# Attention scores by 32 small matmuls instead of 8 padded ones, and a softmax that reads PSUM

## The chip, the cores and the metric

The kernel runs on one core of one Trainium2 chip. The metric is the device time of one execution in microseconds (us). Three executions were timed; times of two kernels that lie within 0.3% of each other (about 3.7 us here) can hardly be told apart.

## What is computed

Chunked attention with memory keys, then two gated feed-forward layers over the same 3072 tokens (4 sequences of 768, 8 heads of 64):

```python
for c in range(nc):                      # chunks of 32 queries
    l_start, r_end = max(0, c_start - 16), min(S, c_end + 8)
    k_full = concat(mem_k, k[l_start:r_end])     # 8 memory keys and up to 56
    scores = scale * q_c @ k_full.T
    a = exp(scores - max(scores)); a = a / (sum(a) + 1e-9)
    out[c] = a @ v_full
x = (sigmoid(x @ w_gate) * (x @ w_val)) @ w_out          # 512 -> 1536 -> 512
h = x @ w_in                                              # 512 -> 2048
g = (a0 + a1*h + a2*h*h + a3*h*h*h) / (1 + |b0|*|h| + |b1|*h*h + 1e-6)
y = g @ w_out2                                            # 2048 -> 512
```

A chunk of 32 queries sees at most 8 + 16 + 32 + 8 = 64 keys (KEYS). Two neighbouring chunks of one sequence share a window of 104 keys (WIN): memory, the context of both, memory again.

## The kernel before

**Tiling.** The tokens are handled in 24 tiles of 128 (index t). A tile has 8 heads and two groups g of 64 queries, each group two chunks. In the kernel before, one "set" is 128 query rows of the scores: for one pair of heads (r, 4 of them) and one g, two chunks c by two heads h by 32 queries. `attn_qk` makes a set with one matmul that contracts 128 rows, two heads of 64 features, over all 104 keys of the window; the host has laid out q so that each query column holds zeros in the other head's rows, so a tile's q is 512 KB. The 8 sets fill two PSUM tiles sp, four sets each. ScalarE then copies from each the 64 keys that belong to a chunk (lines 99 and 100, two copies of 64 rows by 4 x 64 for each PSUM tile) into the SBUF tile s. In the first and last tile of each sequence (every t with t % 6 equal to 0 or 5) GpSimd masks the keys that lie outside it.

**Softmax.** `attn_max` (VectorE: maximum over each 64 keys, then subtraction), `attn_exp` (ScalarE), `attn_sum` and `attn_mul` (VectorE, into a buffer with zeros outside the chunk's keys). `attn_t` transposes the 8 sets (tiles tp), `attn_pv` multiplies by the values in 16 matmuls with 64 weight columns, 64 moving columns and 104 rows (tile xp). All of these are plain float32, which the trace shows as two MATMUL records and two LDWEIGHTS records for each matmul of the source, except the transposes, which have one.

**Feed-forward layers.** They run on blocks of 512 tokens. Each large product is three float32r matmuls (hi by hi, hi by lo, lo by hi): `gate_val` (line 235, tile h), `out1` (line 267, tile acc), `h2` (line 316), `out2` (line 355). Weights arrive as raw 64-bit words, are converted by ScalarE and VectorE and split into hi and lo (`split_hi`, `split_lo`, line 222) during the first block, a step ahead of their use.

**Order.** Everything is written out by hand, and each engine works through its own queue in that order. First comes a prologue (lines 472 to 538): loads on the SyncE queue, attention of tiles 0 to 3, first weights. Then come 72 steps, one for each block j and inner tile f of the first layer: `gate_val` twice, `g_split`, then `attn_qk` and `attn_max` where the plan has them, then `out1` of the step before. Tiles 4 to 23 of attention are spread over these steps, two tiles at a time, and are all done after half of the run. PSUM has four rotating banks (pool ps) for h, sp, tp and xp, and four fixed ones for acc.

Of the kernel before, what the change touches and what calls it, by code (L numbers as in the profile page):

```python
# [39 lines left out]
def fused_kernel(ctx: ExitStack, tc: tile.TileContext, q, k, v, w1, w2, coef, x2d, w2d, out):  # L40
    """Chunked attention with memory keys, then two gated feed-forward layers.

    Float32 operands of the large products are split exactly into two float32r
    parts, hi + lo; each product is hi*hi + hi*lo + lo*hi, accumulated in float32.
    Activations stay transposed (features on partitions), so that each layer's
    result is the next one's moving operand.
    """
    nc = tc.nc
# [14 lines left out]

    # Attention weights between zeros: each chunk's keys within the window of two.
    a_buf = [const.tile([P, NSET, WIN], F32, name=f"a{i}") for i in range(2)]
# [7 lines left out]
    def ps(name):  # L73
        return psp.tile([P, 512], F32, tag="ps", name=name)

# [1 line left out]
    qs, ks, vs, s_sb, at_sb = {}, {}, {}, {}, {}  # L77

    def load_qk(t):
        u = qs[t] = wpool.tile([P, NSET, P], F32, tag="w", name=f"q{t}")  # L80
        nc.sync.dma_start(out=u, in_=q[t])
        u = ks[t] = wpool.tile([P, KW], F32, tag="w", name=f"k{t}")
        nc.sync.dma_start(out=u, in_=k[t])

    def load_v(t):
        u = vs[t] = wpool.tile([P, VW], F32, tag="w", name=f"v{t}")
        nc.sync.dma_start(out=u[0:WIN], in_=v[t])

    def attn_qk(t):
        qt = qs.pop(t)  # L90
        kt = ks.pop(t).rearrange("p (s w) -> p s w", s=NSET)
        s = tpool.tile([P, NSET, KEYS], F32, tag="t", name=f"s{t}")
        for half in range(2):
            sp = ps(f"sp{t}_{half}")[:, 0 : 4 * WIN].rearrange("p (s w) -> p s w", s=4)
            for i in range(4):
                j = 4 * half + i
                nc.tensor.matmul(sp[:, i], lhsT=qt[:, j], rhs=kt[:, j], start=True, stop=True)  # L97
            j = slice(4 * half, 4 * half + 4)
            nc.scalar.activation(out=s[0:64, j], in_=sp[0:64, :, 0:KEYS], func=ACTF.Copy)
            nc.scalar.activation(out=s[64:128, j], in_=sp[64:128, :, OFF1:WIN], func=ACTF.Copy)  # L100
        sv = s.rearrange("p (r g) w -> p r g w", g=2)
        if t % SB == 0:
            nc.gpsimd.memset(sv[0:64, :, 0, NMEM : NMEM + LEFT], MASKED)
        if t % SB == SB - 1:
            e = CTX - RIGHT + NMEM - OFF1
            nc.gpsimd.memset(sv[64:128, :, 1, e : e + RIGHT], MASKED)
        s_sb[t] = s

    def attn_max(t):
        s = s_sb[t]  # L110
        m = spool.tile([P, NSET, 1], F32, tag="m", name=f"m{t}")
        nc.vector.tensor_reduce(out=m[:, :, 0], in_=s, axis=AX.X, op=ALU.max)
        nc.vector.tensor_tensor(out=s, in0=s, in1=m.to_broadcast([P, NSET, KEYS]), op=ALU.subtract)

# [34 lines left out]
    def attn_pv(t, x, n0):  # L149
        vt = vs.pop(t)[0:WIN].rearrange("p (g e) -> p g e", g=2)  # L150
        ats = at_sb.pop(t)
        xp = ps(f"xp{t}").rearrange("p (r n) -> p r n", r=4)
        for j in range(NSET):
            r, g = divmod(j, 2)
            at = ats[j // 4][0:WIN].rearrange("p (s c h q) -> p s h c q", s=4, c=2, h=2)
            for h in range(2):
                e = (2 * r + h) * D
                nc.tensor.matmul(  # L158
                    xp[64 * h : 64 * h + 64, r, 64 * g : 64 * g + 64],
                    lhsT=vt[:, g, e : e + D],  # L160
                    rhs=at[:, j % 4, h],
                    start=True,
                    stop=True,
                )
        hi, lo = x[:, :, 0, n0 : n0 + P], x[:, :, 1, n0 : n0 + P]
        nc.scalar.activation(out=hi, in_=xp, func=ACTF.Copy)  # L166
        nc.vector.tensor_tensor(out=lo, in0=xp, in1=hi.bitcast(F32), op=ALU.subtract)  # L167

# [1 line left out]
    # Float64 arrives as raw 8-byte words and is rounded to float32 here. The high  # L170
    # word, scaled as a float32, has its exponent rebased and in place after a shift
    # by 3; the 3 bits that this frees take the low word, rounded without a carry:
    # within one unit of float32, exact for float32 values, and even on average.
    stage = {}
# [48 lines left out]

    # hi*hi, hi*lo, lo*hi
    TERMS = ((0, 0), (0, 1), (1, 0))

# [1 line left out]
    xt, gp, sgs = {}, {}, {}  # L228
# [57 lines left out]

# [1 line left out]
    x2f, x2, w2f, rat = {}, {}, {}, {}  # L288
# [21 lines left out]
    def h2(j, f):  # L310
        """The rational function's negative, split; the sign goes out with the result."""
        x, w = x2[j], wp[2, 2 * f]
        hp = ps(f"h2_{j}_{f}")
        for kt in range(KT):
            for i, (a, b) in enumerate(TERMS):
                nc.tensor.matmul(  # L316
                    hp,
                    lhsT=w[:, a, kt * P : (kt + 1) * P],
                    rhs=x[:, kt, b],
                    start=(kt == 0 and i == 0),  # L320
                    stop=(kt == KT - 1 and i == 2),
                )
        t, qq, hh = t2(f"t{j}_{f}"), t2(f"qq{j}_{f}"), t2("hh")
        nc.scalar.activation(out=t, in_=hp, func=ACTF.Identity, scale=cf[:, 3:4], bias=cf[:, 2:3])  # L324
        nc.scalar.activation(out=qq, in_=hp, func=ACTF.Abs, scale=cab[:, 0:1])
        nc.scalar.activation(out=hh, in_=hp, func=ACTF.Square)  # L326
        nc.vector.tensor_tensor(out=t, in0=t, in1=hp, op=ALU.mult)  # L327
        nc.vector.scalar_tensor_tensor(out=t, in0=t, scalar=cf[:, 1:2], in1=hp, op0=ALU.add, op1=ALU.mult)  # L328
        nc.vector.scalar_tensor_tensor(out=qq, in0=hh, scalar=cab[:, 1:2], in1=qq, op0=ALU.mult, op1=ALU.add)  # L329
        rat[j, f] = t, qq  # L330

    def recip2(j, f):
        # 1 / Q: the square of 1 / sqrt(Q) from the table, and one Newton step.
        t, qq = rat[j, f]
        y = t2("y")
        nc.scalar.activation(out=y, in_=qq, func=ACTF.Abs_reciprocal_sqrt, bias=qc[:, 0:1])  # L336
        nc.scalar.activation(out=y, in_=y, func=ACTF.Square)  # L337
        rat[j, f] = t, qq, y
# [31 lines left out]

# [1 line left out]
    NB1 = len(BLOCKS1)  # L372
# [45 lines left out]
    def at(si, *call):  # L418
        plan.setdefault(si, []).append(call)

    # Weights of the first layer: scaled three steps ahead, converted two, split one.
    for si, (j, f, c0, n) in enumerate(steps):
# [4 lines left out]
        if j == 0:  # L427
            at(si - 2, bits1, f)
            at(si - 3, scale1, f)
            if f > 2:  # L430
                at(max(si - 3, 0), load_w1, f)
    # Attention of later blocks, two tiles of 128 tokens at a time.
    for t in range(4, NBLK, 2):
        j, i = divmod(t, 4)
        s0 = (j - 1) * NF1 + (5 if i else 0)
        if j == 1:
            s0 = 5 if i else 2
        for o, u in ((0, t), (1, t + 1)):
            at(s0 + o - 2, load_qk, u)
            at(s0 + o, attn_qk, u)  # L440
            at(s0 + o + 1, attn_max, u)
            at(s0 + 3, attn_exp, u)
            at(s0 + o + 3, load_v, u)
            at(s0 + o + 3, attn_sum, u)
            at(s0 + o + 3, attn_mul, u)
            at(s0 + o + 4, attn_t, u)
            at(s0 + o + 5, pv, u)
    # Conversion of the second layer's weights.
    for i in range(2 * NF2):
# [6 lines left out]
    def weights2(k, n):  # L456
        """The next n units are loaded and the ones before split."""
        for i in range(k, k + n):
# [6 lines left out]
    W2_AHEAD = 2  # L465
    # The second layer's first PRE inner tiles come within the first layer's last
    # steps; its second product is LAG2 steps behind its first.
    PRE, LAG2 = 3, 5
    with tc.manual_schedule():
        # The first block's attention and first weights, ordered so that no engine's  # L470
        # queue waits long for another's.
        load_qk(0)
# [122 lines left out]
def _windows(k, mem):  # L595
    """[B, H, S // 64, WIN, D]: memory, the context of two chunks, memory."""
    import numpy as np
# [62 lines left out]
```

## Time and profile before

| | |
|---|---|
| three timed runs, us | 1234.36, 1236.14, 1237.49 (median 1236.14) |
| span of the profiled execution, us | 1234.2 |
| TensorE matmul busy | 1213.6 us (98%) |
| TensorE weight loads busy | 1010.7 us (82%) |
| VectorE busy | 905.8 us (73%) |
| ScalarE busy | 792.8 us (64%) |
| mean granted TensorE clock | 0.995 |

The span runs from the first to the last instruction of the one execution that was profiled, so nothing of its own lies around it but what the timed runs add: the median is 1.9 us above the span. A matmul's record includes its way through a pipeline, so that records overlap; what a matmul costs is read from start to start.

### The profile page before, as it was taken

Reading aid. Unit: us, or ns where it says so; the run is one execution under the profiler, and the core shown is the slowest. Engines: PE = TensorE matmul, PEld = TensorE weight load, DVE = VectorE, ACT = ScalarE, POOL = GpSimd, SP = SyncE. Lnnn points to the kernel's source line nnn. Section 1 sums busy time; section 2 is a strip of 40 time slices with the busy share of each in tenths; the row PEclk is TensorE's granted clock in tenths of the full one; section 3 lists DMA queues with packets and bytes.
Section 4 is the critical chain, followed back from the end, with each engine's and each line's share of the span. In section 5 each row is a group of like instructions: output and inputs, shape, how many; then the busy total and the mean of one; then the engine's idle time right before and its main releaser. Section 6 shows DMA issues by size and latency. Waiting matters only on the chain.

```text
span 1234.2 us, 16440 instructions
## 1 busy us (share of the span) xinstructions
PE 1213.6 (98%) x6240; PEld 1010.7 (82%) x6240; DVE 905.8 (73%) x1426; ACT 792.8 (64%) x1382; POOL 3.3 (0%) x19
## 2 busy tenths in 40 slices
PE   5899999999999999999999999999999999999998
PEld 5788888888888888888888888888888888888887
DVE  5889655747465656556566579998888898898885
ACT  5988455655565555555555588777677677767765
POOL 0000000000000000000000000000000000000000
PEclk8999999999999999999999999999999999999999
DMA  9864151325242514422163120010010100100000
GB/s 320 312 210 148 46 158 52 110 91 175 65 128 86 183 53 141 137 90 79 54 203 94 43 69 18 9 52 9 10 52 9 44 18 9 52 18 1 35 1 35
DMA packets 39319, 105.40 MB, mean 85 GB/s; under 512 B 4488, under 2 KB 4488, under 8 KB 39240
## 3 DMA queue, kind: packets, MB, share of 16 engines
q1 hardware_dynamic: 39240, 104.35, 26.3%
q8 instruction: 49, 0.80, 0.3%
q14 instruction: 30, 0.25, 0.1%
HBM read 83.36 MB, written 20.97 MB: 85 GB/s over the span
## 4 chain that ended last, share of the span: by engine, by line
PE 97%; DMA 1%; ACT 1%; DVE 0%; issue 0%; SPq 0%
PE h L235 32%; PE acc L355 21%; PE h L316 21%; PE acc L267 16%; PE sp L97 3%; PE tp L144 2%; PE xp L158 2%; DMA k<-k_in 1%; DVE x L167 0%; ACT at L146 0%; ACT st L187 0%; ACT st L188 0%; ACT s L117 0%; DVE a L131 0%; DVE r L124 0%
## 5 line engine op out<-in xcount | busy, mean ns | idle before, releaser
L235 PE MATMUL h<-x,wp 128*128 128x512 f32 x1728 | 414.3, 393 | 3.7 <-ACT x L166 3.0
L235 PEld LDWEIGHTS h<-x,wp 128*128 128x128 f32 x1728 | 322.9, 188 | 72.0 <-ACT x L166 3.2
L316 PE MATMUL h<-x,wp 128*128 128x512 f32 x1152 | 276.5, 389 | 0.0
L355 PE MATMUL acc<-wp,g 128*128 128x512 f32 x1152 | 275.9, 389 | 0.0
L355 PEld LDWEIGHTS acc<-wp,g 128*128 128x128 f32 x1152 | 216.3, 188 | 44.8
L316 PEld LDWEIGHTS h<-x,wp 128*128 128x128 f32 x1152 | 216.2, 188 | 44.8
L267 PE MATMUL acc<-g,wp 128*128 128x512 f32 x864 | 210.1, 392 | 0.0
L267 PEld LDWEIGHTS acc<-g,wp 128*128 128x128 f32 x864 | 160.8, 188 | 33.0
L253 ACT ACTIVATE g<-sg 128x512 fp32r<-128x512 f32 x72 | 45.5, 632 | 179.9 <-DVE sg L247 179.9
L324 ACT ACTIVATE t<-h,cf 128x512 f32<-128x512 f32 x96 | 74.7, 778 | 127.9 <-PE h L316 127.0
L222 DVE TENSOR_TENSOR wp<-wf,wp 128x512 fp32r<-128x512 f32 x216 | 136.2, 684 | 5.9 <-ACT wp L218 5.7
L247 DVE TENSOR_TENSOR sg<-sg,h 128x512 f32<-128x512 f32 x72 | 49.5, 687 | 123.8 <-PE h L235 103.6
L218 ACT ACTIVATE wp<-wf 128x512 fp32r<-128x512 f32 x216 | 121.1, 622 | 6.2 <-DVE c L199 4.0
L327 DVE TENSOR_TENSOR t<-t,h 128x512 f32<-128x512 f32 x96 | 65.8, 686 | 45.3 <-ACT hh L326 43.6
L244 ACT ACTIVATE sg<-h 128x512 f32<-128x512 f32 x72 | 43.0, 598 | 75.9 <-PE h L235 75.7
L254 DVE TENSOR_TENSOR g<-sg,g 128x512 fp32r<-128x512 f32 x72 | 49.9, 692 | 52.1 <-ACT g L253 52.1
L328 DVE SCALAR_TENSOR_TENSOR t<-t,cf,h 128x512 f32<-128x512 f32 x96 | 71.8, 748 | 3.4
L342 DVE SCALAR_TENSOR_TENSOR qq<-qq,y 128x512 f32<-128x512 f32 x96 | 65.8, 685 | 11.0 <-ACT y L337 11.0
L336 ACT ACTIVATE y<-qq,qc 128x512 f32<-128x512 f32 x96 | 69.9, 728 | 5.0 <-DVE qq L329 4.7
L329 DVE SCALAR_TENSOR_TENSOR qq<-hh,cab,qq 128x512 f32<-128x512 f32 x96 | 71.7, 746 | 0.0
L343 DVE SCALAR_TENSOR_TENSOR t<-t,cf,y 128x512 f32<-128x512 f32 x96 | 71.5, 745 | 0.0
L344 DVE SCALAR_TENSOR_TENSOR t<-qq,t 128x512 f32<-128x512 f32 x96 | 66.5, 692 | 3.3
(52 smaller groups left out, 1018.0 us busy)
## 6 DMA issues: line engine op xcount, KB each, us to landing
st<-w_in SPq DMA_DIRECT2D x68, 512.0 KB, 8.0
q<-q_in SPq DMA_DIRECT2D x24, 512.0 KB, 12.0
k<-k_in SPq DMA_DIRECT2D x24, 416.0 KB, 7.9
v<-v_in SPq DMA_DIRECT2D x24, 416.0 KB
w2d<-c SPq DMA_DIRECT2D x32, 256.0 KB, 2.1
w2f<-w2d SPq DMA_DIRECT2D x32, 256.0 KB, 3.2
x2d<-x2s SPq DMA_DIRECT2D x24, 256.0 KB, 2.8
x2f<-x2d SPq DMA_DIRECT2D x24, 256.0 KB
```

The source lines that it names most:

```text
L218: nc.scalar.activation(out=wp[key][:, 0], in_=src, func=ACTF.Copy)
L222: nc.vector.tensor_tensor(out=t[:, 1], in0=src, in1=t[:, 0].bitcast(F32), op=ALU.subtract)
L235: nc.tensor.matmul(pt, lhsT=w[:, a, kt * P : (kt + 1) * P], rhs=x[:, kt, b, c0 : c0 + n], start=(kt == 0 and i == 0), stop=(kt == KT - 1 a ...
L267: nc.tensor.matmul(acc[j][d][:, c0 : c0 + n], lhsT=w[:, a, d * P : (d + 1) * P], rhs=g[:, b, 0:n], start=(f == 0 and c0 == 0 and i == 0), ...
L316: nc.tensor.matmul(hp, lhsT=w[:, a, kt * P : (kt + 1) * P], rhs=x[:, kt, b], start=(kt == 0 and i == 0), stop=(kt == KT - 1 and i == 2),)
L324: nc.scalar.activation(out=t, in_=hp, func=ACTF.Identity, scale=cf[:, 3:4], bias=cf[:, 2:3])
L328: nc.vector.scalar_tensor_tensor(out=t, in0=t, scalar=cf[:, 1:2], in1=hp, op0=ALU.add, op1=ALU.mult)
L329: nc.vector.scalar_tensor_tensor(out=qq, in0=hh, scalar=cab[:, 1:2], in1=qq, op0=ALU.mult, op1=ALU.add)
L336: nc.scalar.activation(out=y, in_=qq, func=ACTF.Abs_reciprocal_sqrt, bias=qc[:, 0:1])
L343: nc.vector.scalar_tensor_tensor(out=t, in0=t, scalar=cf[:, 0:1], in1=y, op0=ALU.add, op1=ALU.mult)
L344: nc.vector.scalar_tensor_tensor(out=t, in0=qq, scalar=2.0, in1=t, op0=ALU.subtract, op1=ALU.mult)
L355: nc.tensor.matmul(acc[j][m], lhsT=g[:, a, m * P : (m + 1) * P], rhs=w[:, b], start=(f == 0 and i == 0), stop=(f == NF2 - 1 and i == 2),)
```

## The change

A set is now one chunk index of the tile by one head: 128 rows are (c, g, 32 queries), four strips of 32. `attn_qk` issues, for each head pair r, chunk strip i and head h, one matmul that contracts only the 64 rows of that head (rows 64h on), has 32 weight columns (the chunk's queries) and 64 moving columns (the chunk's own keys), and writes 32 partitions of the PSUM tile of that h. That is 32 matmuls for a tile in place of 8. The layout of q needs no zeros and halves to 256 KB for a tile.

In the 16 tiles that need no mask, `attn_max` reads both PSUM tiles directly: two maxima and two subtractions of 128 x 256 in place of one of each of 128 x 512, and the four ScalarE copies are gone. In the 8 tiles with a mask, two copies of 128 x 256 remain. `attn_max` of the later tiles stands in the step of their `attn_qk`, one step earlier than before. `attn_pv` issues the same 16 matmuls, in an order of loops that follows the new sets. Comments were dropped.

```diff
-        for half in range(2):
-            sp = ps(f"sp{t}_{half}")[:, 0 : 4 * WIN].rearrange("p (s w) -> p s w", s=4)
-            for i in range(4):
-                j = 4 * half + i
-                nc.tensor.matmul(sp[:, i], lhsT=qt[:, j], rhs=kt[:, j], start=True, stop=True)
-            j = slice(4 * half, 4 * half + 4)
-            nc.scalar.activation(out=s[0:64, j], in_=sp[0:64, :, 0:KEYS], func=ACTF.Copy)
-            nc.scalar.activation(out=s[64:128, j], in_=sp[64:128, :, OFF1:WIN], func=ACTF.Copy)
+        sps = [ps(f"sp{t}_{h}")[:, 0 : 4 * KEYS].rearrange("p (r w) -> p r w", r=4) for h in range(2)]
+        for r in range(4):
+            for i in range(4):
                 c, g = divmod(i, 2)
+                for h in range(2):
+                    d = slice(64 * h, 64 * h + 64)
+                    o = slice(32 * i, 32 * i + 32)
+                    nc.tensor.matmul(
+                        sps[h][o, r],
+                        lhsT=qt[d, r, o],
+                        rhs=kt[d, r, g, c * OFF1 : c * OFF1 + KEYS],
+                        start=True,
+                        stop=True,
+                    )
...
+        if edge(t):
+            for h in range(2):
+                nc.scalar.activation(out=sv[:, :, h], in_=sps[h], func=ACTF.Copy)
...
+        else:
+            sc_ps[t] = sps
...
+        for h in range(2):
+            nc.vector.tensor_reduce(out=mv[:, :, h, 0], in_=sps[h], axis=AX.X, op=ALU.max)
+        for h in range(2):
+            nc.vector.tensor_tensor(
+                out=sv[:, :, h], in0=sps[h], in1=mv[:, :, h].to_broadcast([P, 4, KEYS]), op=ALU.subtract
+            )
...
-            at(s0 + o + 1, attn_max, u)
+            at(s0 + o, attn_max, u)
```

On TensorE, around tile 4 (names: h_2 is `gate_val` of inner tile f = 2, acc is `out1` of the step before), this stood before:

```order
L235 MATMUL h_2_0_0_584<-x_280,wp_0_2_0_494 128x512 x12
L235 MATMUL h_2_1_0_602<-x_280,wp_0_2_1_496 128x512 x12
L97 MATMUL sp_0_626<-k_427,q_425 128x104 x4
L97 MATMUL sp_1_633<-k_427,q_425 128x104 x4
L267 MATMUL acc_0_548<-g_0_1_0_545,wp_0_1_2_433 128x512 x3
```

and this stands there now, with sp_0 and sp_1 taking turns 32 times where the dots are:

```order
L261 MATMUL h_2_0_0_672<-x_368,wp_0_2_0_582 128x512 x12
L261 MATMUL h_2_1_0_690<-x_368,wp_0_2_1_584 128x512 x12
L104 MATMUL sp_0_713<-k_515,q_513 32x64
L104 MATMUL sp_1_714<-k_515,q_513 32x64
...
L293 MATMUL acc_0_636<-g_0_1_0_633,wp_0_1_2_521 128x512 x3
```

The block stands at the same place; only its form is another.

On VectorE, in the prologue (tiles 1 and 2; m is the maximum, r the reciprocal sum, s the scores), this stood before:

```order
L112 TENSOR_REDUCE m_197<-s_163 128x8
L113 TENSOR_TENSOR s_163<-s_163,m_197 128x512
L112 TENSOR_REDUCE m_201<-s_178 128x8
L113 TENSOR_TENSOR s_178<-s_178,m_201 128x512
L124 TENSOR_REDUCE r_204<-s_163 128x8
```

and this stands there now:

```order
L135 TENSOR_REDUCE m_259<-sp_0_185 128x4
L135 TENSOR_REDUCE m_259<-sp_1_186 128x4
L137 TENSOR_TENSOR s_219<-sp_0_185,m_259 128x4x64
L137 TENSOR_TENSOR s_219<-sp_1_186,m_259 128x4x64
L135 TENSOR_REDUCE m_265<-sp_0_220 128x4
L135 TENSOR_REDUCE m_265<-sp_1_221 128x4
L137 TENSOR_TENSOR s_254<-sp_0_220,m_265 128x4x64
L137 TENSOR_TENSOR s_254<-sp_1_221,m_265 128x4x64
L150 TENSOR_REDUCE r_270<-s_219 128x8
```

VectorE now waits for TensorE itself there, in place of ScalarE's copies, and has four instructions for two.

## Rows read from the trace of the kernel before

**Rows 1.** The page: engines, and shares of the chain that ended last.
```profile
PE 1213.6 (98%) x6240; PEld 1010.7 (82%) x6240; DVE 905.8 (73%) x1426; ACT 792.8 (64%) x1382; POOL 3.3 (0%) x19
PE 97%; DMA 1%; ACT 1%; DVE 0%; issue 0%; SPq 0%
```

**Rows 2.** Busy time by stretch: start:end and length, each engine, PEclk, DMA share, GB/s.
```profile
0.00:20.00 20.00, 10.71 (x62) 10.60 (x62) 8.08 (x15) 7.84 (x17) 2.33 (x12) 0.93 0.91 319
40.00:100.00 60.00, 60.00 (x297) 50.23 (x297) 53.56 (x91) 53.69 (x98) 0.27 (x2) 0.99 0.69 234
140.00:600.00 460.00, 460.00 (x2643) 384.23 (x2642) 269.98 (x439) 254.84 (x456) 0.66 (x5) 1.00 0.33 104
```

**Rows 3.** Timeline of TensorE, 141 to 172 us: start, length, instructions merged.
```profile
141.83 2.88 PE L235 MATMUL h<-x,wp 128*128 128x512 f32 x12
144.64 1.15 PE L158 MATMUL xp<-at,v 104*64 104x64 f32 x32
145.72 3.02 PE L235 MATMUL h<-x,wp 128*128 128x512 f32 x12
148.57 2.88 PE L267 MATMUL acc<-g,wp 128*128 128x512 f32 x12
151.29 5.60 PE L235 MATMUL h<-x,wp 128*128 128x512 f32 x24
156.74 1.93 PE L97 MATMUL sp<-k,q 128*128 128x104 f32 x16
158.44 3.01 PE L267 MATMUL acc<-g,wp 128*128 128x512 f32 x12
161.29 5.60 PE L235 MATMUL h<-x,wp 128*128 128x512 f32 x24
```

**Rows 4.** The same timeline from 135 us, eight transposes and what follows them.
```profile
135.42 1.08 PE L144 MATMUL tp<-ident,a 128*104 128x128 f32 x8
136.26 3.01 PE L235 MATMUL h<-x,wp 128*128 128x512 f32 x12
```

**Rows 5.** TensorE's busy time and granted clock (PEclk, third) in three early stretches.
```profile
24.08:25.25 1.17, 1.17 (x32) 1.00 1.03 406
31.08:34.10 3.02, 3.02 (x97) 1.00 1.03 409
17.20:20.83 3.63, 3.63 (x18) 0.53 1.07 397
```

**Rows 6.** Timeline of TensorE in the first 60 us.
```profile
17.20 3.63 PE L97 MATMUL sp<-k,q 128*128 128x104 f32 x16 [3.72 <-DMA k<-k_in]
38.34 12.52 PE L235 MATMUL h<-x,wp 128*128 128x512 f32 x47 [0.73 <-DVE x L167]
```

**Rows 7.** Timeline of VectorE, 10 to 30 us; in brackets the idle time before.
```profile
10.21 0.69 DVE L112 TENSOR_REDUCE m<-s 128x8 f32<-128x512 f32 x1 [10.21 <-ACT s L100]
13.12 0.17 DVE L125 TENSOR_SCALAR r<-r 128x8 f32<-128x8 f32 x1
13.99 0.69 DVE L112 TENSOR_REDUCE m<-s 128x8 f32<-128x512 f32 x1 [0.46 <-ACT s L100]
15.58 0.69 DVE L112 TENSOR_REDUCE m<-s 128x8 f32<-128x512 f32 x1 [0.17 <-ACT s L100]
21.67 0.69 DVE L112 TENSOR_REDUCE m<-s 128x8 f32<-128x512 f32 x1 [0.97 <-ACT s L100]
23.44 0.69 DVE L124 TENSOR_REDUCE r<-s 128x8 f32<-128x512 f32 x1 [0.36 <-ACT s L117]
25.07 0.69 DVE L124 TENSOR_REDUCE r<-s 128x8 f32<-128x512 f32 x1 [0.50 <-ACT s L117]
26.12 2.75 DVE L131 TENSOR_TENSOR a<-s,r 64x512 f32<-64x512 f32 x4
```

**Rows 8.** The chain that ended last, its longest transfer; then ScalarE's copies by line.
```profile
5.45 11.62 DMA k<-k_in
...
L100 ACT ACTIVATE s<-sp 64x256 f32<-64x256 f32 x48 | 18.2, 380 | 0.6
```

More of the change, by code (lines that the diff above doesn't have):

```diff
@@ L74, in ps @@
         return psp.tile([P, 512], F32, tag="ps", name=name)
-    qs, ks, vs, s_sb, at_sb = {}, {}, {}, {}, {}
+    qs, ks, vs, s_sb, sc_ps, at_sb = {}, {}, {}, {}, {}, {}
     def load_qk(t):
-        u = qs[t] = wpool.tile([P, NSET, P], F32, tag="w", name=f"q{t}")
+        u = qs[t] = wpool.tile([P, 4, P], F32, tag="w", name=f"q{t}")
         nc.sync.dma_start(out=u, in_=q[t])
@@ L87, in load_v, with edge @@
         nc.sync.dma_start(out=u[0:WIN], in_=v[t])
+    def edge(t):
+        return t % SB in (0, SB - 1)
     def attn_qk(t):
         qt = qs.pop(t)
-        kt = ks.pop(t).rearrange("p (s w) -> p s w", s=NSET)
-        s = tpool.tile([P, NSET, KEYS], F32, tag="t", name=f"s{t}")
-        for half in range(2):
-            sp = ps(f"sp{t}_{half}")[:, 0 : 4 * WIN].rearrange("p (s w) -> p s w", s=4)
+        kt = ks.pop(t).rearrange("p (r g w) -> p r g w", r=4, g=2)
+        sps = [ps(f"sp{t}_{h}")[:, 0 : 4 * KEYS].rearrange("p (r w) -> p r w", r=4) for h in range(2)]
+        for r in range(4):
             for i in range(4):
-                j = 4 * half + i
-                nc.tensor.matmul(sp[:, i], lhsT=qt[:, j], rhs=kt[:, j], start=True, stop=True)
-            j = slice(4 * half, 4 * half + 4)
-            nc.scalar.activation(out=s[0:64, j], in_=sp[0:64, :, 0:KEYS], func=ACTF.Copy)
-            nc.scalar.activation(out=s[64:128, j], in_=sp[64:128, :, OFF1:WIN], func=ACTF.Copy)
[L101 to L107, printed above, removed]
+                c, g = divmod(i, 2)
+                for h in range(2):
[8 more added lines that the diff above has]
+                    )
+        s = s_sb[t] = tpool.tile([P, NSET, KEYS], F32, tag="t", name=f"s{t}")
+        sv = s.rearrange("p (r h) w -> p r h w", h=2)
+        if edge(t):
+            for h in range(2):
+                nc.scalar.activation(out=sv[:, :, h], in_=sps[h], func=ACTF.Copy)
+            if t % SB == 0:
+                nc.gpsimd.memset(s[0:32, :, NMEM : NMEM + LEFT], MASKED)
+            else:
+                e = CTX - RIGHT + NMEM - OFF1
+                nc.gpsimd.memset(s[96:128, :, e : e + RIGHT], MASKED)
+        else:
+            sc_ps[t] = sps
     def attn_max(t):
@@ L111, in attn_max @@
         m = spool.tile([P, NSET, 1], F32, tag="m", name=f"m{t}")
-        nc.vector.tensor_reduce(out=m[:, :, 0], in_=s, axis=AX.X, op=ALU.max)
-        nc.vector.tensor_tensor(out=s, in0=s, in1=m.to_broadcast([P, NSET, KEYS]), op=ALU.subtract)
+        if edge(t):
+            nc.vector.tensor_reduce(out=m[:, :, 0], in_=s, axis=AX.X, op=ALU.max)
+            nc.vector.tensor_tensor(out=s, in0=s, in1=m.to_broadcast([P, NSET, KEYS]), op=ALU.subtract)
+            return
+        sv = s.rearrange("p (r h) w -> p r h w", h=2)
+        mv = m.rearrange("p (r h) w -> p r h w", h=2)
+        sps = sc_ps.pop(t)
+        for h in range(2):
[4 more added lines that the diff above has]
+            )
     def attn_exp(t):
@@ L152, in attn_pv @@
         xp = ps(f"xp{t}").rearrange("p (r n) -> p r n", r=4)
[L153 to L164, printed above, removed]
+        for r in range(4):
+            at = ats[r // 2][0:WIN].rearrange("p (s c g q) -> p s g c q", s=4, c=2, g=2)
+            for g in range(2):
+                for h in range(2):
+                    e = (2 * r + h) * D
+                    nc.tensor.matmul(
+                        xp[64 * h : 64 * h + 64, r, 64 * g : 64 * g + 64],
+                        lhsT=vt[:, g, e : e + D],
+                        rhs=at[:, 2 * (r % 2) + h, g],
+                        start=True,
+                        stop=True,
+                    )
         hi, lo = x[:, :, 0, n0 : n0 + P], x[:, :, 1, n0 : n0 + P]
@@ L613 @@
     a = {n: np.asarray(x) for n, x in inputs.items()}
-    q = a["q"].reshape(B, 4, 2, SB, 2, 2, CH, D).transpose(0, 3, 2, 7, 1, 4, 5, 6)
-    qd = np.zeros((B, SB, 2, D, 4, 2, 2, 2, CH), q.dtype)
-    for h in range(2):
-        qd[:, :, h, :, :, :, :, h] = q[:, :, h]
+    qd = a["q"].reshape(B, 4, 2, SB, 2, 2, CH, D).transpose(0, 3, 2, 7, 1, 5, 4, 6)
     kd = _windows(a["k"], a["mem_k"]).reshape(B, 4, 2, SB, 2, WIN, D)
@@ L635 @@
     arrays = {
-        "q_in": qd.reshape(NBLK, P, NSET, P),
+        "q_in": qd.reshape(NBLK, P, 4, P),
         "k_in": kd.reshape(NBLK, P, KW),
```

## The prediction

> **What bounds the kernel now.** I read the page's engine lines and the chain that ended last first: TensorE is busy for 98% of the span and has 97% of that chain [rows 1]. Then the busy time by stretch: from 40 us on TensorE has no gap (60.00 of 60.00, 460.00 of 460.00), while VectorE and ScalarE are busy for 53.6 and 53.7 of 60 us up to 100 us, and for little over half of the time after it [rows 2]. So two stages have different rules. In the prologue, up to 38.34 us, where the dense matmuls start [rows 6], transfers and then VectorE and ScalarE set the pace. After it, what TensorE spends per attention tile is added to the time, and what the other engines save is worth nothing. Twenty of the 24 tiles have their scores in that second stage, so the price of a score block on TensorE, start to start, is the first thing to work out.
>
> **The price of a score block before.** Dense work alone: 24 h matmuls start at 151.29 and the sp block at 156.74, so 5.45 us for 24, or 0.227 us each [rows 3]. From 151.29 to 161.29 there are 24 h, one sp block and 12 acc: 10.00 - 36 x 0.227 = 1.83 us for one sp block with its changes of form. Inside it 16 records take 156.74 to 158.44, 0.106 us each. A record has 128 weight columns and 104 moving ones. A transpose has 104 weight columns and 128 moving ones and costs (136.26 - 135.42) / 8 = 0.105 us [rows 4]. So a column costs about 0.83 ns in float32 on either side, loading and streaming overlap, and the larger of the two sets the pace.
>
> **The price after.** No row has a matmul of 64 rows and 32 columns. The nearest is xp: 64 weight columns and 64 moving ones, into alternating halves of the output partitions, two records for each matmul, as the new one. Three blocks in a row, 96 records, cost 3.02 us and one block of 32 costs 1.17, both at the full clock (granted 1.00, the 2.4 GHz level) [rows 5]; the 97th record counted there is the end of the one before: (3.02 - 1.17) / 64 = 28.9 ns a record, 57.8 ns a matmul. By 0.83 ns a column one record streams for 53 ns, two 107 ns; a matmul that adds only 58 therefore overlaps half of itself with its neighbour. I read this as: the second record of a matmul must wait until the first has streamed its 64 columns through the same part of the array (53 ns), the next matmul, in another part, starts a few ns after the second, and starts keep their order. The whole xp block, from 141.83 to 148.57 with 24 h around it, costs 6.74 - 5.45 = 1.29 us [rows 3], so 1.29 - 16 x 0.0578 = 0.37 us go into entering and leaving the small form.
>
> The new block has the same 64 moving columns and the same pair of records on the same part of the array; only its neighbours are spread over eight parts and not two, and its load is 32 columns, which was not the slower side. If starts keep their order the eight parts help no more than two do. I take 57.8 ns: 32 x 0.0578 + 0.37 = 2.22 us in place of 1.83, +0.39 us a tile, **+7.8 us** for 20 tiles. The matmul count grows fourfold, and the work per matmul falls by less.
>
> Bounds for that price. From below, full independence of the eight parts: each has 4 matmuls of two records, 8 x 53 ns = 0.43 us, and 0.79 us with the 0.37, -1.04 a tile. From above, each load and stream one after the other, 27 + 53 ns a record: 64 x 0.080 + 0.37 = 5.5 us, +3.7 a tile; the xp rows, which would then cost 107 ns a record, speak plainly against that. For entering and leaving, sp itself shows that it can be less (1.83 - 16 x 0.106 = 0.13 us for the 128-column form) and nothing shows that it can be more; that gives +0.15 to +0.39 a tile at the same rate.
>
> **The prologue.** There the change helps. The chain before runs through the arrival of tile 3's k at 17.07 (5.45 + 11.62) [rows 8]. Four q of 512 KB lie ahead of it in the queue, and now four of 256 KB: 1.05 MB less, at 319 GB/s (mean of 0 to 20 us [rows 2]) to 406 GB/s [rows 5] 2.6 to 3.3 us earlier. Whether VectorE can use it: before its last multiplications for tiles 2 and 3 (26.12) it idled, after its first maximum at 10.21, for 0.46, 0.17, 0.97, 0.36 and 0.50 us behind ScalarE's copies or the exponentials that were queued behind them [rows 7], 2.46 us together; the first k comes 0.6 us earlier too (256 KB at 406 GB/s). For tiles 1 to 3 the copies go (four of 0.38 us each tile [rows 8]) and with them those waits. Against that stand four VectorE instructions for two in three tiles. A 128 x 512 reduction takes 0.69, an instruction on 128 x 8 0.17 [rows 7], so half the size is about 0.43: 4 x 0.43 - 2 x 0.69 = 0.34, 1.0 us for three tiles. Sum 0.6 + 2.46 - 1.0 = 2.1 us, a little under what the transfers offer; **-2.1 us**. The bounds are 0 (ScalarE's conversions of weights, nearly continuous there, hold the end of the prologue) and -4 (the transfers' 3.3 and part of the saved copies). TensorE's clock adds noise: tile 3's scores ran almost wholly at the 1.2 GHz level (granted 0.53 from 17.20 to 20.83 [rows 5]), at 0.227 us a record (3.63 / 16), after a wait of 3.72 us [rows 6], and where such stretches fall may move.
>
> **What costs nothing.** In the steps ScalarE loses 1.5 us a tile in 13 unmasked tiles and VectorE gains 0.34; both lie under TensorE's dense work [rows 2]. `attn_max` now holds two of the four rotating PSUM banks until VectorE has read them, and stands in the queue behind `g_split`. Behind it stand the conversions and the lo parts of later weights. The banks it holds are asked for by the next tile's scores or transposes, a step (36 x 0.227 = 8.2 us of matmuls) later, so there is room. If VectorE were later than that, TensorE would wait for a bank, some tenths of a us in each of the steps from 53 to 100 us, where VectorE's cover is only 6.4 us in 60.
>
> **Sum.** The three runs' median, 1236.1, is 1.9 us above the profiled span of 1234.2; I add to the median: 1236.1 + 7.8 - 2.1 = **1241.8 us** (a span near 1239.9).
>
> **Rivals.** (1) *Eight parts overlap, faster.* For it: the two halves of xp do overlap. Against it: if parts were free of each other, xp's two would each need 107 ns per matmul and so give 53, which is within 5 ns of what is seen, so the rows do not rule it out as firmly as I should like; that is why it keeps a chance. With the eight parts free: 1236.1 - 20.8 - 2.1 = 1213 us. A milder form, in which the load of 64 columns paced xp and 32 columns halve it: 32 x 0.0289 + 0.37 = 1.29, -0.54 a tile, 1223 us. It turns my sign when a matmul costs under 49 ns ((1.83 + 2.1 / 20 - 0.37) / 32), measurably so under 43. The Trainium skill (TensorE: Matmul & The Clock Gate, Part 3) gives a rule of this kind: tiles in different parts of the array run together, and each further one adds about 4 ns to the span of one; nothing in this trace has more than two parts in turn.
>
> (2) *A load waits for the stream before it, much slower.* If the load for a matmul's second record cannot run under the first record's stream, as both use the same rows, a matmul costs 53 + 27 + 6 = 86 ns: 32 x 0.086 + 0.37 = 3.12 us, +1.29 a tile, 1260 us. Against it: in xp every load uses the same rows as the stream before, and 28.9 ns a record leaves no room for it. The Trainium skill (same page and part) says that a weight load overlaps a running matmul only where the row group differs; the rows of xp disagree with it here.
>
> (3) *No change that can be measured.* The small form is entered as cheaply as sp's was (+0.15 a tile, +3 us) or the prologue gives its full 4 us: 1235 to 1240. For it: the two terms have opposite signs. Under 0.3%, 3.7 us, this measurement cannot tell it from nothing.
>
> **Numbers.** Chances: 60% for my sum (own range 1238 to 1247), 14% for rival 1 (8 for 1213, 6 for 1223), 10% for rival 2, 16% for rival 3. Of my own case a sixth lies under 1239.8. So slower by over 0.3%: 0.50 + 0.10 = 0.60; same: 0.10 + 0.15 = 0.25; faster: 0.15. The range 1223 to 1253 leaves out the freest form of rival 1 and rival 2, under 2 in 10.
>
> **What would show it.** In the profile after, a score block should start 64 records at a mean of about 29 ns and take 2.2 us with what it adds to its neighbours; 27 ns or less for a whole matmul, or a block under 1.3 us, means rival 1; over 80 ns per matmul, rival 2. The dense h matmuls should begin near 36.2 us in place of 38.34. TensorE should show no gap after that; a wait of sp, tp or h on VectorE's line 137 would make me wrong about the banks, and an h start at 38 or later about the prologue.

## The result, and the profile after

The changed kernel took 1221.65 us (median of four runs, 1218.23 to 1222.83) against 1236.02 for the kernel before on the same chip: a ratio of 0.988, with a 95% interval of 0.9863 to 0.9897. The forecast was 1241.8, slower, in a range from 1223 to 1253; the time lies below that range. Two repeats of the changed kernel on later occasions gave 1220.82 against 1236.73 and 1221.76 against 1236.28, so the gain is 14.4 to 15.9 us. The profiled execution was the fastest of its four: 1218.23 us, span 1216.5.

The page after, engines and shares of the chain that ended last, answers to [rows 1]:

```profile
PE 1193.0 (98%) x7392; PEld 981.5 (81%) x7392; DVE 906.7 (75%) x1458; ACT 760.5 (63%) x1302; POOL 3.5 (0%) x19
PE 89%; DVE 5%; ACT 3%; DMA 2%; issue 1%; SPq 0%; POOL 0%; DVEq 0%; POOLq 0%; ACTq 0%
```

TensorE still bounds the kernel, with 20.6 us less to do, but 8% of the chain now runs through VectorE and ScalarE. The timeline of TensorE after, the same place as [rows 3] (start, length, then weight rows*columns and moving rows x columns; instructions merged):

```profile
146.25 5.60 PE L261 MATMUL h<-x,wp 128*128 128x512 f32 x24
151.78 0.86 PE L104 MATMUL sp<-k,q 64*32 64x64 f32 x64
152.56 3.06 PE L293 MATMUL acc<-g,wp 128*128 128x512 f32 x12
155.46 5.60 PE L261 MATMUL h<-x,wp 128*128 128x512 f32 x24
```

Read it as the prediction read the kernel before: from 146.25 to 155.46 are 9.21 us, of which 36 x 0.227 = 8.17 are dense; the score block adds 1.04 us where 2.22 were forecast and 1.83 were paid before. From the start of the block to the start of what follows, 64 records take 0.78 us, where 16 took 1.70.

In the first 45 us TensorE's timeline after shows what holds the prologue now (brackets: idle before, and what ended it):

```profile
15.32 1.28 PE L104 MATMUL sp<-k,q 64*32 64x64 f32 x64 [4.59 <-DMA k<-k_in]
28.01 3.36 PE L184 MATMUL xp<-at,v 104*64 104x64 f32 x64 [2.17 <-DMA v<-v_in]
34.08 13.11 PE L261 MATMUL h<-x,wp 128*128 128x512 f32 x47 [0.30 <-DVE x L193]
```

Dense work starts at 34.08 in place of 38.34 [rows 6], tile 3's scores at 15.32 in place of 17.20, and a transfer that nobody waited for before, v of tile 2, is waited for at 28 us. TensorE's waits from 34 us to the end (us, times, longest) show that it is no longer free of gaps:

```profile
PE tp L170 <- DVE s L137: 1.0, 1, 1.0
PE h L261 <- ACT sg L270: 0.6, 1, 0.6
PE h L261 <- DVE x L193: 0.3, 1, 0.3
```

**Where the time came from.** I cut the span at two places: the start of the 47 dense matmuls and the start of tile 8's scores (151.78 after, 156.74 before [rows 3]). From that second cut on, 16 tiles remain.

| us | start of dense work | from there to tile 8's scores | from tile 8's scores to the end |
|---|---|---|---|
| before | 38.34 | 118.40 | 1077.5 |
| changed, profile of the first run | 34.08 | 117.70 | 1064.7 |
| changed, two later profiles (runs e8 and e12 below) | 37.37, 36.99 | 117.66, 117.67 | 1064.2, 1064.7 |

The last column gives 12.8 us for 16 tiles, 0.80 us each, which is what the timeline shows for a block (1.83 - 1.04 = 0.79). The middle column should have given 4 x 0.79 = 3.2 us and gave 0.7: the 47 matmuls took 0.6 us longer (13.11 against 12.52, at a mean granted clock of 0.82 against 0.89) and new gaps took the waits above. The first column differs by 3 us between executions of the same kernel, and that is most of the scatter of its times.

### The profile page after: what moved, and what is told of

Read it like the earlier page. It is cut to its first block, busy times and chain, and to the rows that moved or that the text cites. A ratio compares the mean times of both kernels' runs of the same rounds, so it can differ in the third digit from the quotient of the medians.

```text
span 1216.5 us, 18667 instructions
## 1 busy us (share of the span) xinstructions
PE 1193.0 (98%) x7392; PEld 981.5 (81%) x7392; DVE 906.7 (75%) x1458; ACT 760.5 (63%) x1302; POOL 3.5 (0%) x19
## 4 chain that ended last, share of the span: by engine, by line
PE 89%; DVE 5%; ACT 3%; DMA 2%; issue 1%; SPq 0%; POOL 0%; DVEq 0%; POOLq 0%; ACTq 0%
PE h L261 28%; PE acc L381 21%; PE h L342 21%; PE acc L293 14%; PE xp L184 2%; PE tp L170 1%; DVE wf L218 1%; DVE wp L248 1%; DVE wf L225 1%; PE sp L104 1%; DMA v<-v_in 1%; DMA st<-w_in 1%; ACT g L279 1%; DVE sg L273 0%; ACT wp L244 0%
```

## The experiments

**How parts of the array overlap: four orders of the same 32 matmuls.** Only the loops around the matmul differ, and so how many parts (row half h, strip i) take turns. The kernels write each order as one loop over a list; it is shown here as nested loops.

```diff
-        for r in range(4):
-            for i in range(4):
-                for h in range(2):
+        # e1: one part at a time
+        for i in range(4):
+            for h in range(2):
+                for r in range(4):
+        # e2: two row halves of one strip
+        for i in range(4):
+            for r in range(4):
+                for h in range(2):
+        # e3: two strips of one row half
+        for r, i, h in [(r, 2 * p + i, h) for h in range(2) for p in range(2) for r in range(4) for i in range(2)]:
+        # e4: four strips of one row half
+        for h in range(2):
+            for r in range(4):
+                for i in range(4):
```

> The 32 score matmuls of a tile in an order that gives four in turn to the same part of the array (row half and strip) before the next part is used; otherwise the changed kernel. Theory P, every part works through its own records at 53 ns each and only different parts overlap: 107 ns a matmul, a block adds 32 x 0.107 + 0.37 = 3.8 us against 1.04 in the changed kernel, about 50 us more in all. Theory L, the load of 32 weight columns sets the pace wherever it goes: a block stays near 1.04 us and the time where it is.

> The order gives matmuls in turn to two parts, the two row halves of one strip. Theory P: 53 ns a matmul, a block adds 1.7 + 0.37 = 2.1 us, about 20 us more in all, the sum that the prediction had for eight parts. Theory L: 1.04 us a block, no change. If row halves did not overlap at all: 3.8 us, as with one part.

> The order gives matmuls in turn to two parts, two strips of 32 output partitions of one row half, as the value product does with its two halves. Theory P: 2.1 us a block, as with two row halves. Theory L: 1.04 us a block. If strips of one row half shared the stream of rows: 3.8 us.

> The order gives matmuls in turn to four parts, the four strips of one row half, then of the other. Theory P: 27 ns a matmul, a block adds 0.86 + 0.37 = 1.2 us, about 4 us more in all. Theory L: 1.04 us a block.

One execution of each: 1248.68, 1228.32, 1227.75 and 1219.09 us, beside 1238.23 for the kernel before. The timelines of TensorE at tile 8, one fence for each kernel in that order:

```profile
151.97 5.60 PE L259 MATMUL h<-x,wp 128*128 128x512 f32 x24
157.50 2.40 PE L102 MATMUL sp<-k,q 64*32 64x64 f32 x64
159.83 3.06 PE L291 MATMUL acc<-g,wp 128*128 128x512 f32 x12
162.73 5.60 PE L259 MATMUL h<-x,wp 128*128 128x512 f32 x24
```

```profile
152.92 1.42 PE L102 MATMUL sp<-k,q 64*32 64x64 f32 x64
154.26 3.06 PE L291 MATMUL acc<-g,wp 128*128 128x512 f32 x12
```

```profile
152.83 1.42 PE L102 MATMUL sp<-k,q 64*32 64x64 f32 x64
154.18 3.02 PE L291 MATMUL acc<-g,wp 128*128 128x512 f32 x12
```

```profile
151.43 0.99 PE L102 MATMUL sp<-k,q 64*32 64x64 f32 x64
152.35 3.02 PE L291 MATMUL acc<-g,wp 128*128 128x512 f32 x12
```

Start to start the block takes 2.33 us with one part at a time, 1.34 and 1.35 with two, 0.92 with four and 0.78 with eight. The work is the same to the last column, so the load of 32 columns does not set the pace (theory L falls): the number of parts in turn does. Which two parts it is, row halves or strips, makes no difference, and neither does the target of the writes: the two parts of e2 write to two PSUM tiles, those of e3 to one. With one part at a time the change would have made the kernel slower (1248.68 against 1238.23).

Theory P is right in kind, and its sizes are too large: with the change of form a block adds 2.59, 1.60, 1.56 and 1.14 us (from the 24 h before it to the h behind it in the same timelines, less 8.17), where it gave 3.8, 2.1, 2.1 and 1.2. The whole times scatter with the start of dense work (e4's begins at 33.63 us, as early as in the changed kernel's fastest run, which puts it below that kernel's median), but from tile 8's scores to the end the four took 1089.4, 1073.6, 1073.1 and 1065.9 us beside 1064.7 for the changed kernel, as 16 blocks of these prices make it, to within 0.4 us.

The reason can be read from e1: if starts kept the program's order, each part's 8 records would start over 7 x 53 = 0.37 us before the next part could begin, and eight parts would take 3.0 us; 2.33 means that the next part begins while the one before still has records to start. The Trainium skill (TensorE: Matmul & The Clock Gate, Part 3) says that matmuls start and end in program order, without reordering; by that rule e1 would be near 3.0, and the 2.33 measured here speaks against it for the starts on different parts. The Trainium skill's rule in the same part, that tiles packed into different parts run together, is borne out.

The starts of e1's single records show it directly. Counted from the block's first, they are 0, 80, 135, 191, 247, 253, 303, 333, 359, 389, 415, 445 ns and so on: one series of eight records, about 56 ns apart after the first step of 80, and a second series of the same form that begins 6 ns after the fifth record of the first. A new series begins every 253 ns, and there are eight of them, as there are parts. Two windows from the block's start (start:end, length, busy, records; then granted clock and transfers) show the fifth and sixth record together:

```profile
157.50:157.74 0.24, 0.24 (x4) 1.00 0.00 0
157.50:157.76 0.26, 0.26 (x6) 1.00 0.00 0
```

**Another order of the eight parts.**

```diff
-            for i in range(4):
-                for h in range(2):
+            for h in range(2):
+                for i in range(4):
```

> The changed kernel with the eight parts taken in another order, four strips of one row half and then four of the other, again for each r. Theory P, only the number of parts in turn counts: the block stays at 0.79 us start to start and the time where it is. Rival, neighbours that share a strip hinder each other: below 0.75 us a block, 1 us or more in all.

1220.82 us (1220.08 to 1223.67), ratio to before 0.9876 (0.9858 to 0.9893), against 1221.76 for the changed kernel beside it. Its timeline shows the same price, 0.79 us here and 0.78 above by rounding:

```profile
153.64 0.86 PE L104 MATMUL sp<-k,q 64*32 64x64 f32 x64
154.43 3.06 PE L293 MATMUL acc<-g,wp 128*128 128x512 f32 x12
```

With eight parts in turn, these two orders cost the same. Eight parts take 0.78 us where 8 x 56 ns = 0.45 would be parts wholly free of each other. The changed kernel's windows from the block's start show where they lose it:

```profile
151.78:151.83 0.05, 0.05 (x8) 1.00 0.00 0
151.78:152.03 0.25, 0.25 (x32) 1.00 0.00 0
151.78:152.10 0.32, 0.32 (x34) 1.00 0.00 0
151.78:152.57 0.79, 0.79 (x64) 1.00 0.00 0
```

The first 32 records start at the parts' own pace, in four rounds of eight (at 0, 80, 136 and 192 ns, inside a round 5 to 9 ns apart). Then only two start in 0.07 us, and the other 30 follow about 10 ns apart, the last at 0.64 us. What holds them back from the middle of the block on was not tried and is not shown.

**The matmuls alone, without the direct reading of PSUM (run e5, beside e8).**

```diff
-        if edge(t):
+        if True:
             for h in range(2):
                 nc.scalar.activation(out=sv[:, :, h], in_=sps[h], func=ACTF.Copy)
...
-            at(s0 + o, attn_max, u)
+            at(s0 + o + 1, attn_max, u)
```

> The changed kernel with ScalarE's two copies of 128 x 256 kept for every tile, the softmax from SBUF and its maximum one step after the scores, as before: the matmuls and the halved q alone. Theory T, what TensorE saves per tile makes most of the gain: 0.79 us for each of 16 tiles after the first block stays, 12.6 us, and the transfers' part of the prologue too, so a time of 1220 to 1224 us; dense matmuls start 1 to 2 us later than the 34.08 us of the changed kernel, and the wait of 1.0 us for a bank near 99 us is gone. Rival S, the softmax's direct reading makes the gain: the time goes back by most of 14 us, to 1230 or more.

> The changed kernel itself, for comparison on the same chip: 1218 to 1223 us, dense matmuls from 34 us on.

1221.09 us (1217.63 to 1222.45), ratio 0.9873 (0.9855 to 0.989), beside 1220.82 (1220.49 to 1221.59), ratio 0.9875 (0.9859 to 0.9892), for the changed kernel on the same chip: no difference that can be told. Theory S falls. In the profiles dense work starts at 38.55 (37.37 in e8), the first block takes 116.8 us to tile 8's scores (117.7), and the rest the same 1064.2. So the direct reading costs 0.8 us in the first block; the 1.2 us by which dense work starts earlier with it in this pair of profiles is within what the prologue scatters. The wait for a bank is gone, as the list of e5's waits on TensorE after 39 us shows, and the one for the sigmoid is longer:

```profile
PE h L261 <- ACT sg L270: 1.2, 1, 1.2
PE h L261 <- DVE x L193: 0.3, 1, 0.3
```

**The size of q (run e6).**

```diff
-        u = qs[t] = wpool.tile([P, 4, P], F32, tag="w", name=f"q{t}")
+        u = qs[t] = wpool.tile([P, 8, P], F32, tag="w", name=f"q{t}")
```

> The changed kernel with 512 KB loaded for each q again (the second half is never read). Theory Q, transfers set the prologue: 1.05 MB more ahead of tile 3's k and of the first weights, so dense matmuls start 2.6 us or more later than 34.08 us and the time is 2 to 4 us above the changed kernel. Rival: the copies that are gone and VectorE's shorter waits made the prologue shorter; then the start and the time stay within 0.7 us of the changed kernel.

1223.5 us (1222.78 to 1224.01), 2.7 above the changed kernel beside it, whose range it does not touch; on the two other occasions that kernel's runs reach 1222.83 and 1223.74, so the direction is better shown than the size. TensorE's timelines of the wide q and then of the changed kernel (e8):

```profile
33.19 3.68 PE L184 MATMUL xp<-at,v 104*64 104x64 f32 x64 [3.79 <-DMA v<-v_in]
39.59 5.75 PE L261 MATMUL h<-x,wp 128*128 128x512 f32 x17 [0.29 <-DVE x L193]
```

```profile
31.07 3.60 PE L184 MATMUL xp<-at,v 104*64 104x64 f32 x64 [4.06 <-DMA v<-v_in]
37.37 7.88 PE L261 MATMUL h<-x,wp 128*128 128x512 f32 x26 [0.59 <-DVE x L193]
```

In this pair everything shifts by 2.1 to 2.2 us behind one transfer, which is less than the 3.3 us by which profiles of the changed kernel differ among themselves. It fits a prologue that runs at the pace of the queue of loads, as the early v below shows more clearly; by the times the halved q can be worth all that the prologue gains.

**VectorE in the first block (run e7).**

```diff
-            nc.vector.tensor_tensor(
+            (nc.gpsimd if t >= 4 else nc.vector).tensor_tensor(
                 out=a[lo : lo + 64, :, c0 : c0 + KEYS],
```

> The changed kernel with attn_mul of tiles 4 and later on GpSimd in place of VectorE, which spares VectorE 1.4 us a tile. Theory V, VectorE's queue in the first block takes back 1.8 us: the gaps of TensorE near 99 and 130 us (1.1 and 0.7 us) go, and the time is about 2 us lower than the changed kernel. Rival: GpSimd is slower, the transposes wait for it and the time rises, by more than 2 us if each of 20 tiles waits only 0.1 us.

1220.44 us (1220.2 to 1221.07), ratio 0.9872 (0.9858 to 0.9887): 0.4 below e8, with ranges that overlap. In its profile the gaps are gone; this is all that TensorE waits for after 39 us, and under it GpSimd's group for line 157 (busy, mean ns):

```profile
PE h L261 <- DVE x L193: 0.3, 1, 0.3
...
L157 POOL TENSOR_TENSOR a<-s,r 64x512 f32<-64x512 f32 x40 | 42.1, 1054 | 320.7 <-DVE r L152 280.1 <-ACT at L172 27.0 <-PE h L261 12.2
```

The first block takes 116.2 us and not 117.7, so theory V holds for the gaps: 1.5 us. The time does not show it. The profile's dense work began 1.5 us later (38.85), so that the spans are equal at 1219.3. GpSimd is slower (1054 ns for what took VectorE 0.69 us) and no one waits for it.

**The load that is late (run e9), and both (e10, beside e12).**

```diff
         load_v(3)
+        load_v(2)
         nc.sync.dma_start(out=cf, in_=coef)
         load_w1(1)
-        load_v(2)
```

> The changed kernel with the load of v for tile 2 issued before the second set of weights in place of behind it. In the profiles of the changed kernel TensorE waits 2.2 to 4.1 us for that v, which lands near 28 to 31 us, and the x of the first block waits for its product. Theory D, this transfer now holds the end of the prologue: the wait goes and the time is 1.5 to 3 us lower than the changed kernel. Rival: ScalarE's conversions or the later weights hold it as well, and the time stays within 0.7 us.

> The early v and attn_mul of tiles 4 and later on GpSimd together. Theory D and V: 1.5 to 3 us from the prologue and about 1.8 us from the gaps of the first block, 3 to 5 us under the changed kernel, and no gap of TensorE after the first dense matmul. Rival: VectorE falls behind in another place and the two do not add up; then it is no better than the early v alone.

> The changed kernel itself, for comparison on the same chip: 1218 to 1223 us.

The early v: 1217.9 us (1217.58 to 1218.22), ratio 0.9848 (0.9832 to 0.9865). Both: 1215.83 (1215.59 to 1216.87), ratio 0.9833 (0.9818 to 0.9847). The changed kernel beside them: 1221.76 (1221.11 to 1223.74), ratio 0.9882 (0.9866 to 0.9897). So the load is worth 3.9 us, and its slowest run is as fast as the fastest of the changed kernel's twelve (1218.23). GpSimd takes off 2.1 more on top of it, though alone it showed only 0.4. This is the fastest version of the study, 20.4 us under the kernel before. TensorE's timeline with both:

```profile
25.84 3.02 PE L184 MATMUL xp<-at,v 104*64 104x64 f32 x96
32.06 0.49 PE L261 MATMUL h<-x,wp 128*128 128x512 f32 x1 [3.20 <-ACT x L192]
33.30 12.77 PE L261 MATMUL h<-x,wp 128*128 128x512 f32 x47 [0.74 <-DVE x L193]
```

No transfer stands before the products of tiles 1 to 3 any more; they run on, and what is waited for is ScalarE. Dense work starts at 33.30, and tile 8's scores 116.1 us later. One gap is left, 0.3 us for a bank.

## Why the prediction was wrong

- **What bounds the kernel, and the price before** (1.83 us a block): right. The method, start to start with the dense work taken off, gave the block after as well, and 16 tiles at 0.79 us add up to 12.6 of the 12.8 us seen.
- **The price after is the step that failed**: "the second record of a matmul must wait until the first has streamed ..., the next matmul, in another part, starts a few ns after the second, and starts keep their order", so that "the eight parts help no more than two do". The runs show in its place that each part streams its own records at its own pace (one every 56 ns in e1), that other parts go on meanwhile, and that a later part may start before an earlier one has started all of its own. xp at 57.8 ns a matmul was not an order of starts with a small step between; it was two parts at once, each starting a record every 58 ns. The prediction wrote that down in rival 1 ("if parts were free of each other, xp's two would each need 107 ns per matmul and so give 53") and gave it 14%, though two readings that differ by 5 ns in the only row that was read called for even chances. They differ by a factor of four as soon as eight parts are in turn. The 1.18 us between 2.22 and 1.04, for 20 tiles, are 23.6 us.

  The trace of the kernel before could have settled it. Inside the xp block at 144.64 us [rows 3] the single records start at 0, 7, 107, 113, 165, 172, 223, 230 ns and so on, in pairs from the first on. By the prediction's reading the first record would start alone and the second 53 ns after it. Three windows of that block:

```profile
144.64:144.65 0.01, 0.01 (x2) 1.00 0.00 0
144.64:144.74 0.10, 0.10 (x2) 1.00 0.00 0
144.64:144.76 0.12, 0.12 (x4) 1.00 0.00 0
```

- **Rival 1's own sizes**: the free form said 0.79 us a block and 1213 us in all. The block came to 1.04, with 0.26 for entering and leaving in place of 0.37 but 0.78 for its records in place of 0.43, and the first block took back another 1.7 us in gaps; 1221.65 lies near its milder form, but not by its mechanism, which e1 to e4 refute.
- **Rival 2**, a load that waits for the stream before it: refuted, by the block after (86 ns a matmul would be 3.12 us).
- **The prologue**, -2.1 us: right in size, and in part by luck. Of the 14.4 to 15.9 us in all, 12.8 and 0.7 belong to the later columns of the table, which leaves 0.9 to 2.4; single profiles show 1.0 to 4.3, beside the one profile of the kernel before (dense work from 34.08 to 37.37 us, where 36.2 was forecast). The transfers, which the prediction named as the bound, fit (up to 2.7 us for the halved q). The 2.46 us of VectorE's waits that make up most of the sum are not borne out: keeping the copies (e5) did not lengthen the time measurably. That v of tile 2 would be late next was not foreseen.
- **VectorE's instructions**: 0.43 us was forecast for half the size. The groups after, for lines 137 and 135, show it:

```profile
L137 DVE TENSOR_TENSOR s<-sp,m 128x256 f32<-128x256 f32 x32 | 12.0, 416 | 0.0
L135 DVE TENSOR_REDUCE m<-sp 128x4 f32<-128x256 f32 x32 | 12.0, 416 | 0.0
```

- **"What costs nothing"**: right from tile 8 on and not before it. The condition that was named, banks of PSUM held by a VectorE that is late, came true once. VectorE's timeline after, just ahead of TensorE's transposes:

```profile
98.84 0.69 DVE L280 TENSOR_TENSOR g<-sg,g 128x512 fp32r<-128x512 f32 x1 [0.70 <-ACT g L279]
99.45 0.75 DVE L135 TENSOR_REDUCE m<-sp 128x4 f32<-128x256 f32 x2
100.11 0.75 DVE L137 TENSOR_TENSOR s<-sp,m 128x256 f32<-128x256 f32 x2
```

```profile
100.67 1.05 PE L170 MATMUL tp<-ident,a 128*104 128x128 f32 x8 [1.01 <-DVE s L137]
```

The scores of the tile had been ready since about 92.9 (their block starts at 92.02 and its records take 0.86 us); VectorE came to them 6.6 us later, and the transposes needed a bank that they held. TensorE had become faster, while VectorE's load there did not fall (53.58 us of 40 to 100 us, 53.56 before [rows 2]), and so TensorE came to wait for it; with attn_mul taken off VectorE (e7) the wait is gone. The row after:

```profile
40.00:100.00 60.00, 59.66 (x532) 48.23 (x530) 53.58 (x93) 48.56 (x88) 0.34 (x2) 1.00 0.67 224
```

## What to carry to other kernels

Small float32 matmuls that take turns among several parts of the array (row half by strip of output partitions) overlap, and the gain grows with the number of parts in turn: here one, two, four and eight parts took 2.33, 1.34, 0.92 and 0.78 us for the same work; so let the innermost loops walk over the parts. A merged row with two parts in turn could not tell an order of starts from free parts; the starts of its single records could. Where two readings fit a row and differ in what is asked, look inside the row, and give them even chances until something tells them apart. When the bounding engine gets faster, look again at what is late next: here one load moved up the queue and one operation given to an idle engine took off 5.9 us more, beside the 14.5 us of the change.

## What was not expected of the hardware

- Two row halves of a strip and two strips of a row half overlap equally well: 1.34 and 1.35 us a block.
- A part's records do not have to have started before a later part's begin: one part at a time took 2.33 us where strict order gives 3.0, and a new part began 6 ns after the fifth of eight records of the one before.
- The same kernel's prologue differed by 3.3 us between two profiled executions (dense work from 34.08 and 37.37 us), with the arrival of one v as the visible difference (TensorE's wait for it ended at 28.01 and at 31.07), while everything from tile 8 on agreed within 0.5 us.
